# Three weight loads of the boot wait for matmuls, and ten more spare matmuls stand at its head

## The chip, the cores and the metric

The kernel runs on one core of a Trainium2 chip. The metric is the time of one execution in microseconds (us); lower is better. A core has five engines with queues of their own: PE (matmuls, with weight loads listed as PEld), DVE and ACT (elementwise work), POOL, and SP, which here only issues DMAs. Each engine works through its queue in order.

## The reference

Two layers follow each other: a recurrence over tokens with a decaying state (4 batches, 8 heads, 768 tokens, 48 channels a head), and a dense layer with the activation h - tanh(h) on its 3072 x 384 result.

```python
for t in range(S):                       # attention, per batch and head
    cur = einsum('bhd,bhe->bhde', u * k[t], v[t])
    y[t] = einsum('bhd,bhde->bhe', r[t], state + cur)
    state = w[t][:, None] * state + einsum('bhd,bhe->bhde', k[t], v[t])
x = y as (3072, 384)
h = x @ w_in                             # (384, 2048)
out = (h - tanh(h)) @ w_out              # (2048, 384)
```

## The kernel before

The tokens are split into eight blocks of 384 (four batches, two halves each). A block's recurrence is done in chunks of 64 tokens: running products of w ahead of and behind each token (pre and post, scans on DVE), scores inside a chunk (matmuls of 64 x 64, masked into the tile A), keys turned so that tokens lie on partitions (turn: PE transposes, then a copy to ks on ACT), updates of the state (update_1 on PE, update_2 on DVE), and results from scores and from states. The result, transposed, is xT, the input of the dense layer. The dense layer's hidden width is cut into 16 slices f of 128. While PE does the slices of block i, the engines prepare block i+1 in the gaps.

The order of work on PE, DVE, ACT and SP is written out by hand (a manual schedule); each engine takes its instructions in the order of the code, and waits are set where data flow from one engine to another. Only the first block has nothing to run beside: the function boot prepares it alone, and the main loop begins behind it.

In boot, SP issues in this order: w, k and r of both halves of the heads, v, then weight tiles. A weight tile is one slice f of w_in and w_out, 768 KB as 64-bit words. load_weights brings it into one of five raw buffers; convert makes three ACT operations of it (one to w_sb, two to up, all on L255) and one DVE operation (L259). more_weights issues the next load and puts it in the list raws, from which convert takes them in order. The first two tiles' ACT operations are run whole ahead of the results; of the third, two are run ahead of the copies of the results and one behind the first copies. begin_behind(ins, dma) makes a DMA wait for an instruction: the queue that issues it (SP) stops there until the instruction is done, and so do the DMAs behind it in that queue.

The steps of boot that matter, in the order of the code: six loads, v and three weight loads (L965 to L970); the first half's products, its turn and scores; the second half's; update_1 (L521, 96 matmuls); ACT's conversion of the first tile, with the fourth and fifth weight loads behind its third operation; results from the first half's scores (L603, 48 matmuls); update_2 on DVE; conversion of the second tile; results from states (L586) with the remaining scores (L447) between them; two operations of the third tile; copies of the results to late and xT (L636); small DMAs that fill the holes in xT from late (fill_holes, L643, three on SP and three on POOL); the next block's w (behind a copy), a sixth weight load; results from the second half's scores; more copies. Then the main loop begins with hp (L749).

Two helpers put matmuls on PE whose results nobody reads: busy (L269, 128 x 512) and passed (L277, 16 x 16). The argument ahead of turn is the number of the latter ahead of the boot's first transposes.

```python
def passed(to, n):
    by = ident.bitcast(BF16)[:, 0:16]
    for _ in range(n):
        nc.tensor.matmul(to[0:16, 0:16], lhsT=by, rhs=by, start=True, stop=True, skip_group_check=True)
```

Of the kernel before, what the change touches and what calls it, by code (L numbers as in the profile page):

```python
# [50 lines left out]
B, H, S, D = 4, 8, 768, 48  # L51
P = 128
L = 64
# [3 lines left out]
NCP = NCH // 2  # L57
# [63 lines left out]
def kernel(  # L121
# [12 lines left out]
    nc = tc.nc  # L134
# [29 lines left out]
    start = const.tile([P, UP * NCH * LP], F32, name="start", tag="start")  # L164
# [32 lines left out]
    A = const.tile([P, 2, NPAIR, NCP, L], F32, name="scores", tag="scores")  # L197
# [41 lines left out]
    def load_weights(f, queue):  # L239
        raw = conv.tile([P, 2 * DM, 2], I32, name="raw", tag="raw")  # L240
        ins = queue.dma_start(out=raw, in_=weights[f].bitcast(I32).rearrange("p (n two) -> p n two", two=2))
        return f, raw, ins

    def convert(f, raw, _):

        lo, hi = raw[:, :, 0], raw[:, :, 1]
        a = w_sb[:, f, :].bitcast(I32)
        up = conv.tile([P, 2 * DM], I32, name="up", tag="up", bufs=4)  # L250
        low, high = (up.bitcast(t).rearrange("p (n two) -> p n two", two=2)[:, :, i]
                     for i, t in enumerate((U16, F16)))

        def scaled(to, of, scale, bias=0.0):
            return lambda: nc.scalar.activation(out=to, in_=of, func=AF.Copy, scale=scale, bias=bias)  # L255

        return [scaled(a.bitcast(F32), hi.bitcast(F32), HIGH_SCALE), scaled(high, hi.bitcast(F32), SIGN_SCALE),
                scaled(low, lo.bitcast(U32), *LOW)], [
                lambda: nc.vector.scalar_tensor_tensor(out=a, in0=a, scalar=3, in1=up, op0=ALU.logical_shift_left,  # L259
                                                       op1=ALU.bitwise_or)]  # L260

    def scratch(ps):
        return ps.tile([P, 2, BANK], F32, name="att", tag="att")
# [17 lines left out]
    class Block:  # L281
# [177 lines left out]
        def own(self, ps, p0):  # L459
            return self.masked(ps, "k", "r", masks["diagonal"], p0)  # L460

        def earlier(self, ps, p0):
            return self.masked(ps, "post", "pre", masks["above"], p0)
# [41 lines left out]
        def update_1(self, ps):  # L505
            last = self.q == NQ - 1
            for cs in ((0, 1), (2,)):
                kvp = scratch(ps)
                for c in cs:
                    for par in range(2):  # L510
                        self.kv[2 * c + par] = kvp[:, par, (c - cs[0]) * NPAIR * D:(c - cs[0] + 1) * NPAIR * D]
                for p in reversed(range(NPAIR)):
                    for c in cs:
                        for h in range(2):
                            for par in range(2):
                                if last and 2 * c + par == NCH - 1:
                                    continue
                                toks = slice(64 * par, 64 * par + 64)
                                e0 = p * D2 + h * D
                                n0 = ((c - cs[0]) * NPAIR + p) * D  # L520
                                nc.tensor.matmul(kvp[64 * h:64 * h + 64, par, n0:n0 + D],  # L521
                                                 lhsT=self.ks[toks, p, c, 64 * h:64 * h + 64],
                                                 rhs=self.v[toks, c, e0:e0 + D], start=True, stop=True)

        def update_2(self):
            St = states[self.q]
# [66 lines left out]
        def from_scores(self, yp, slots, first, last):  # L593
            for n, slot in slots:
                for p in reversed(slot):
                    for c in range(NCP):
                        for h in range(2):
                            for par in range(2):
                                toks = slice(64 * par, 64 * par + 64)
                                e0 = 64 * (h ^ (p % 2))  # L600
                                f0 = p * D2 + h * D
                                n0 = (n * NCP + c) * L
                                nc.tensor.matmul(yp[p % 2][e0:e0 + D, par, n0:n0 + L],  # L603
                                                 lhsT=self.v[toks, c, f0:f0 + D],
                                                 rhs=A[toks, h, p, c, :],
                                                 start=(first and n == slots[0][0] and c == 0),
                                                 stop=(last and (n, c) == (slots[-1][0], NCP - 1)),
                                                 skip_group_check=True)

        def results(self, ps):  # L610
            self.yp = [scratch(ps) for e in range(2)]
# [2 lines left out]
        def result(self, part, pairs, last=False, more=False, **how):  # L614

            if self.begun and not self.more:
                nc.tensor.wait_ge(fence, len(fences))
            slots = [(p // 2, [x for x in pairs if x // 2 == p // 2]) for p in pairs if p % 2 == 0]  # L620
            getattr(self, part)(self.yp, slots, not self.begun, last, **how)
            self.begun, self.more = True, more
            if not last and not more:
                nc.tensor.drain().then_inc(fence, 1)
                fences.append(None)

        def result_out(self, pairs, copy=None):

# [323 lines left out]
    def more_weights(queue):  # L952
        raws.append(load_weights(more_weights.n, queue))
        more_weights.n += 1
        return raws[-1][-1]
# [3 lines left out]
    def begin_behind(ins, dma):  # L959
        tc.add_manual_dep(dma.ins, ins.ins.name, mybir.DependencyInfo(  # L960
            mybir.DependencyClass.Sync, mybir.DependencyReason.DATA))

    def boot(ps, blk, later):
        h1, h2 = HALVES
        for p0 in HALVES:  # L965
            for name in ("w", "k", "r"):
                blk.load(name, p0, UP)
        blk.load_v()
        for _ in range(3):
            more_weights(nc.sync)  # L970

        def run(ops):
            for op in ops:
                op()

        both = (h1, h1 + 1), (h2, h2 + 1)
        blk.behind(h1, UP)
        blk.take_whole(h1, UP)
        blk.before(h1, UP)
        blk.times_behind(h1, UP)  # L980
        blk.times_u(h1, UP)
        blk.turn(ps, h1, ahead=97)
        own = blk.own(ps, h1)
        blk.times_before(h1, UP)
        earlier = blk.earlier(ps, h1)
        blk.bound(h1)
        blk.bound(h2)
        blk.behind(h2, UP)
        blk.take_whole(h2, UP)
        own()  # L990
        blk.times_behind(h2, UP)
        blk.times_u(h2, UP)
        blk.turn(ps, h2)
        own = blk.own(ps, h2)
        earlier()
        blk.before(h2, UP)
        blk.times_before(h2, UP)
        blk.update_1(ps)
        first_a, first_b = convert(*raws.pop(0))
        second_a, second_b = convert(*raws.pop(0))  # L1000
        third_a, third_b = convert(*raws.pop(0))
        run(first_a[:2])
        begin_behind(first_a[2](), more_weights(nc.sync))
        more_weights(nc.sync)
        own()
        blk.results(ps)
        blk.result("from_scores", both[0])
        blk.update_2()
        run(second_a)
        blk.result("from_states", ALL, cs=(0, 1), more=True)  # L1010
        earlier = blk.earlier(ps, h2)
        run(third_a[:2])
        blk.result("from_states", ALL, cs=(2,))
        earlier()
        idle = scratch(ps)[:, 0]
        busy(idle, 2)
        blk.result_out((3,), nc.scalar.copy)
        blk.fill_holes([nc.sync, nc.gpsimd])
        begin_behind(blk.result_out((2,), nc.scalar.copy), later.load("w"))
        more_weights(nc.sync)  # L1020
        run(first_b)
        blk.result("from_scores", both[1], True)
        busy(idle, 5)
        run(third_a[2:])
        blk.result_out((1,), nc.scalar.copy)
        blk.result_out((0,), nc.vector.tensor_copy)
        later.load("k")
        fourth_a, fourth_b = convert(*raws.pop(0))
        run(fourth_a[:1])
        run(second_b)  # L1030
        run(third_b)
        blk.held(0, NPAIR)
        return fourth_a[1:], fourth_b
# [24 lines left out]
    for i, blk in enumerate(blocks):  # L1058
# [11 lines left out]
        phases, before, ahead, converted, loads = plan(i)  # L1070
# [3 lines left out]
        for f in range(NF):  # L1074
# [5 lines left out]
            h, made = first(here, f, ps_d)  # L1080
# [75 lines left out]
            while due and due[0][0] <= now:  # L1156
                _, add, what = due.pop(0)
# [84 lines left out]
```

## Time and profile before

| | us |
|---|---|
| median of three runs | 567.99 (567.37 to 569.71) |
| the profiled execution | 567.05 |
| its span, first to last instruction | 565.2 |
| PE busy | 546.4 (97%) |
| DVE busy | 477.3 (84%) |
| ACT busy | 376.8 (67%) |
| first hp matmul of the main loop starts | 27.87 |

Busy times count each engine's own instructions; DMA issues and waits are not counted. A line such as "16.67 0.81 ACT w_sb L255" in the chain of waits gives start, duration, engine, the tile written and the line of the code; the chain is followed back from the last instruction, at each step to whatever released it. In the timeline the text in square brackets is the engine's idle time before the row and what ended it. A tile's view ends with the times from issue to landing of the DMAs that write it. The three weight loads of the boot are issued from 4.5 to 7.2 us and land at about 14, 16 and 18 us; the fourth and fifth are issued at 19.4 and 19.8.

### The profile page before, as it was taken

The page shows a single profiled execution, that of the slowest core. Times are in us where ns is not written, and L with a number is a line of the kernel's source. Part 1 is how long each engine was busy: PE and PEld are TensorE (multiplying, and loading weights), DVE is VectorE, ACT ScalarE, POOL GpSimd, SP SyncE. Part 2 cuts the span into 40 slices and gives each one's busy share as a digit, 9 for nine tenths or more (in the row PEclk, how much of TensorE's full clock was granted, in tenths as well). Part 3 has the DMA queues.
Part 4 walks back from the last instruction along what each step waited for, and adds up shares of the span by engine and source line. Part 5 has one row for each costly group of instructions (what it writes and reads, how often), then busy time and mean ns, then how long its engine had stood idle before and what let it go on. Part 6 is the DMA issues. An engine that isn't in the chain of part 4 may idle for free.

```text
span 565.2 us, 13965 instructions
## 1 busy us (share of the span) xinstructions
PE 546.4 (97%) x5664; PEld 398.3 (70%) x5664; DVE 477.3 (84%) x926; ACT 376.8 (67%) x743; POOL 11.8 (2%) x40
## 2 busy tenths in 40 slices
PE   4889999999999999999999999999999999999996
PEld 4646666565665787877777777877877787787863
DVE  8888884799879989989999999989899998758673
ACT  3979893355337886588766886677865886566450
POOL 6100000000000000000000000000000000000000
PEclk9999999999999999999999999999999999999999
DMA  8596553244202532035302531126122320100101
GB/s 305 198 337 210 182 174 119 84 112 106 92 12 97 131 111 67 4 97 143 112 22 76 140 114 60 52 86 156 57 68 81 83 64 1 55 1 1 44 0 45
DMA packets 51268, 55.10 MB, mean 97 GB/s; under 512 B 21376, under 2 KB 49152, under 8 KB 51200
## 3 DMA queue, kind: packets, MB, share of 16 engines
q1 hardware_dynamic: 50960, 54.10, 31.6%
q8 instruction: 45, 0.74, 0.5%
q14 instruction: 23, 0.19, 0.1%
q0 software_dynamic: 96, 0.07, 0.1%
q10 hardware_dynamic: 144, 0.00, 0.0%
HBM read 43.55 MB, written 4.72 MB: 85 GB/s over the span
## 4 chain that ended last, share of the span: by engine, by line
PE 87%; DVE 6%; ACT 3%; DMA 2%; issue 1%; SPq 0%; DVEq 0%
PE hp L749 40%; PE acc L864 20%; PE acc L826 13%; PE att L864 5%; PE att L447 3%; PE att L586 2%; PE att L603 2%; PE att L521 2%; DVE g L796 1%; ACT up L255 1%; DMA r<-in_rT 1%; DMA w<-in_wT 1%; PE att L471 1%; DVE g L755 1%; DVE post L401 1%
## 5 line engine op out<-in xcount | busy, mean ns | idle before, releaser
L749 PE MATMUL hp<-xT,w_sb 128*128 128x384 f32 x768 | 270.1, 488 | 2.0 <-ACT h L752 1.4
L749 PEld LDWEIGHTS hp<-xT,w_sb 128*128 128x128 f32 x768 | 138.4, 190 | 81.8 <-ACT h L752 4.5
L752 ACT ACTIVATE h<-hp 128x384 f32<-128x384 f32 x128 | 62.8, 490 | 116.4 <-PE hp L749 114.7
L864 PE MATMUL acc<-forms,g 128*128 128x128 f32 x810 | 121.0, 277 | 0.5
L864 PEld LDWEIGHTS acc<-forms,g 128*128 128x128 f32 x810 | 109.1, 192 | 16.9 <-issue 1.2
L796 DVE TENSOR_TENSOR g<-g 128x256 f32<-128x256 f32 x225 | 95.4, 424 | 19.1 <-PE acc L864 0.5
L755 DVE SCALAR_TENSOR_TENSOR h<-h,s 128x384 f32<-128x384 f32 x128 | 70.3, 549 | 7.2 <-ACT s L770 6.6
L826 PE MATMUL acc<-w_sb,sums 128*128 128x384 f32 x192 | 68.1, 491 | 1.4 <-DVE sums L755 1.1
L755 DVE SCALAR_TENSOR_TENSOR g<-qa,h 128x384 f32<-128x384 f32 x96 | 53.6, 558 | 16.2 <-PE acc L864 2.7
L771 ACT ACTIVATE qa<-s,shift 128x384 f32<-128x384 f32 x90 | 55.4, 616 | 3.0
L773 ACT ACTIVATE junk<-s,shift 128x384 bf16<-128x384 f32 x90 | 54.0, 599 | 0.0
L826 PEld LDWEIGHTS acc<-w_sb,sums 128*128 128x128 f32 x192 | 35.7, 190 | 25.8 <-DVE sums L755 2.2
L770 ACT ACTIVATE s<-h 128x384 f32<-128x384 f32 x90 | 47.1, 523 | 2.8
L864 PE MATMUL acc<-w_sb,g 128*128 128x128 f32 x270 | 44.9, 275 | 0.0
L864 PEld LDWEIGHTS acc<-w_sb,g 128*128 128x128 f32 x270 | 37.4, 192 | 0.0
L781 ACT ACTIVATE qa<-s,shift 128x384 f32<-128x384 f32 x38 | 23.4, 617 | 19.3 <-DVE top L778 19.3
L255 ACT ACTIVATE up<-raw 128x768 f16<-128x768 f32 (+1 forms) x32 | 32.0, 1070 | 0.0
L755 DVE SCALAR_TENSOR_TENSOR sums<-qa,h 128x384 f32<-128x384 f32 x32 | 17.9, 558 | 15.6 <-ACT qa L781 12.4
L778 DVE CUSTOM_DVE_ANT_0 s<-h 128x384 f32<-128x384 f32 x38 | 21.0, 553 | 11.7 <-ACT h L752 11.7
L864 PE MATMUL att<-w_sb,g 128*128 128x128 f32 x180 | 30.2, 275 | 0.0
L864 PEld LDWEIGHTS att<-w_sb,g 128*128 128x128 f32 x180 | 26.4, 192 | 4.5
L387 DVE TENSOR_TENSOR_SCAN post<-w,seed 128x780 f32<-128x780 f32 x16 | 28.5, 1783 | 0.7 <-DMA w<-in_wT 0.6
(90 smaller groups left out, 549.3 us busy)
## 6 DMA issues: line engine op xcount, KB each, us to landing
raw<-in_weights SPq DMA_DIRECT2D x16, 768.0 KB, 4.4
w<-in_wT SPq DMA_DIRECT2D x7, 780.0 KB, 4.5
k<-in_kT SPq DMA_DIRECT2D x7, 768.0 KB, 4.4
r<-in_rT SPq DMA_DIRECT2D x7, 768.0 KB, 4.4
v_sb<-in_v SPq DMA_DIRECT2D x8, 576.0 KB, 4.3
k<-in_tokens SPq DMA_DIRECT2D x6, 576.0 KB, 3.9
r<-in_tokens SPq DMA_DIRECT2D x6, 576.0 KB, 4.8
out_y<-sums SPq DMA_DIRECT2D x15, 128.0 KB, 1.9
```

Source lines behind the costliest of these rows:

```text
L255: return lambda: nc.scalar.activation(out=to, in_=of, func=AF.Copy, scale=scale, bias=bias)
L387: return nc.vector.tensor_tensor_scan(out=back(t[:, 0:width]), data0=back(self.tile("w")[:, a:a + width]), data1=back(seed[:, 0:width]), i ...
L749: nc.tensor.matmul(hp, lhsT=w_in_sb[:, f, kc, :], rhs=xT[kc], start=(kc == KC - 1), stop=(kc == 0))
L752: return h, nc.scalar.activation(out=h, in_=hp, func=AF.Copy, scale=1.0 / UPSCALE)
L755: return lambda: nc.vector.scalar_tensor_tensor(out=out, in0=in0, scalar=scalar, in1=in1, op0=op0, op1=ALU.mult)
L770: nc.scalar.activation(out=s, in_=h, func=AF.Square)
L771: nc.scalar.activation(out=qa, in_=s, func=AF.Square, bias=shift[:, 4:5])
L773: nc.scalar.activation(out=junk[:, 0:NB], in_=s, func=AF.Relu, bias=shift[:, 5:6], accum_out=excess[:, at:at + 1])
L781: first = [lambda: nc.scalar.activation(out=qa, in_=s, func=AF.Square, bias=shift[:, 4:5])]
L796: return lambda: nc.vector.tensor_tensor(out=G[:, to:to + 2], in0=two(G, g_at(q, a0), g_at(q, a1)), in1=two(G, g_at(q, b0), g_at(q, b1)), ...
L826: nc.tensor.matmul(acc, lhsT=g[:, j * P:(j + 1) * P], rhs=w_out_sb[:, f, :], start=(f == self.first), stop=(f == NF - 1))
L864: nc.tensor.matmul(to, lhsT=G[:, g_at(q, a), :], rhs=rhs, start=start, stop=stop, skip_group_check=True)
```

## The change

The third weight load is no longer issued with the first two. It waits for the last matmul of update_1. The fourth waits for the last matmul of the results from the first half's scores, and the fifth follows it without a wait of its own; before, these two stood behind the third ACT operation on the first tile. To have something to wait for, update_1, from_scores and result return their last matmul. The spare matmuls ahead of the first turn are 107 instead of 97. The order of the instructions on ACT, DVE, POOL and SP stays as it was; on PE the ten matmuls and their weight loads are added at the head.

```diff
@@ update_1
-    nc.tensor.matmul(kvp[64 * h:64 * h + 64, par, n0:n0 + D], ...)
+    done = nc.tensor.matmul(
+        kvp[64 * h:64 * h + 64, par, n0:n0 + D], ...)
+            return done
@@ from_scores
-    nc.tensor.matmul(yp[p % 2][e0:e0 + D, par, n0:n0 + L], ...)
+    done = nc.tensor.matmul(
+        yp[p % 2][e0:e0 + D, par, n0:n0 + L], ...)
+            return done
@@ result
-            getattr(self, part)(self.yp, slots, not self.begun, last, **how)
+            done = getattr(self, part)(self.yp, slots, not self.begun, last, **how)
...
+            return done
@@ boot
-        for _ in range(3):
+        for _ in range(2):
             more_weights(nc.sync)
...
-        blk.turn(ps, h1, ahead=97)
+        blk.turn(ps, h1, ahead=107)
...
-        blk.update_1(ps)
+        updated = blk.update_1(ps)
         first_a, first_b = convert(*raws.pop(0))
         second_a, second_b = convert(*raws.pop(0))
+        begin_behind(updated, more_weights(nc.sync))
         third_a, third_b = convert(*raws.pop(0))
-        run(first_a[:2])
-        begin_behind(first_a[2](), more_weights(nc.sync))
-        more_weights(nc.sync)
+        run(first_a)
         own()
         blk.results(ps)
-        blk.result("from_scores", both[0])
+        begin_behind(blk.result("from_scores", both[0]), more_weights(nc.sync))
+        more_weights(nc.sync)
         blk.update_2()
         run(second_a)
```

More of the change, by code (lines that the diff above doesn't have):

```diff
@@ L520, in update_1 @@
                                 n0 = ((c - cs[0]) * NPAIR + p) * D
-                                nc.tensor.matmul(kvp[64 * h:64 * h + 64, par, n0:n0 + D],
-                                                 lhsT=self.ks[toks, p, c, 64 * h:64 * h + 64],
-                                                 rhs=self.v[toks, c, e0:e0 + D], start=True, stop=True)
+                                done = nc.tensor.matmul(
+                                    kvp[64 * h:64 * h + 64, par, n0:n0 + D],
+                                    lhsT=self.ks[toks, p, c, 64 * h:64 * h + 64],
+                                    rhs=self.v[toks, c, e0:e0 + D], start=True, stop=True)
+            return done
         def update_2(self):
@@ L602, in from_scores @@
                                 n0 = (n * NCP + c) * L
[L603 to L608, printed above, removed]
+                                done = nc.tensor.matmul(
+                                    yp[p % 2][e0:e0 + D, par, n0:n0 + L], lhsT=self.v[toks, c, f0:f0 + D],
+                                    rhs=A[toks, h, p, c, :], start=(first and n == slots[0][0] and c == 0),
+                                    stop=(last and (n, c) == (slots[-1][0], NCP - 1)), skip_group_check=True)
+            return done
         def results(self, ps):
```

## The prediction

> **What bounds the kernel now.** I read the page first, then the chain of waits from 14 to 42 us, then the timeline of the engines over the same stretch, then the landings of the weight loads. The page gives the frame:
>
> ```profile
> span 565.2 us, 13965 instructions
> ...
> PE 546.4 (97%) x5664; PEld 398.3 (70%) x5664; DVE 477.3 (84%) x926; ACT 376.8 (67%) x743; POOL 11.8 (2%) x40
> ...
> PE 87%; DVE 6%; ACT 3%; DMA 2%; issue 1%; SPq 0%; DVEq 0%
> ```
>
> PE carries the span, and from 42 us to the end its waits that the profile names add up to about 2 us. So the main loop can neither absorb nor return much. What the boot does to the moment at which PE gets steady work is passed on one to one. The edit touches only the boot, and there PE does not lead. Chain of waits, 14 to 42 us (start, duration, what):
>
> ```profile
> 15.87 0.80 ACT ks L473
> 16.67 0.81 ACT w_sb L255
> 17.48 1.88 ACT up L255 x2
> 19.36 0.74 ACT w_sb L255
> 20.10 1.88 ACT up L255 x2
> 21.98 0.78 ACT w_sb L255
> 22.76 0.96 ACT up L255
> 23.73 0.32 ACT late L636
> ...
> 27.29 4.54 DMA w<-in_wT
> 31.83 0.02 issue
> 31.85 1.79 DVE post L387
> ```
>
> The reader should see that from 15.87 to 27.29 us the chain is ACT and nothing else: the copy of the keys, three operations for the first weight tile, three for the second, two for the third, then the copies of the result. They stand in ACT's queue in this order, so a wait of one holds all that follow. The third tile's first operation is the row of 21.85 us in ACT's timeline, and it has no idle time before it: its load had landed long ago (at 6.7 us issued, 11.5 us to landing, so 18.2). PE's timeline shows what the changed loads will wait for:
>
> ```profile
> 15.77 1.56 PE L447 MATMUL att<-r,k 48*64 48x64 f32 x48
> 17.10 2.76 PE L521 MATMUL att<-v_sb,ks 64*64 64x48 f32 x96
> 19.64 1.46 PE L603 MATMUL att<-scores,v_sb 64*48 64x64 f32 x48
> ...
> 22.11 0.90 PE L447 MATMUL att<-pre,post 48*64 48x64 f32 x48
> ...
> 23.59 0.60 PE L269 MATMUL att<-ident 128*128 128x512 bf16 x2
> 24.59 0.55 PE L603 MATMUL att<-scores,v_sb 64*48 64x64 f32 x24 [0.40 <-ACT late L636]
> ```
>
> The updates (L521) end at 17.10 + 2.76 = 19.86 us, the first scores' results (L603) at 19.64 + 1.46 = 21.10. The last thing needed is how long a 768 KB weight load takes when the queue is quiet; tile raw, window 42 to 80 us, eight loads:
>
> ```profile
> DMA to landing us min/median/max: 3.9/4.2/4.3
> ```
>
> **The third load.** Its issue moves from 6.7 us to behind the last L521 matmul. The fourth load of before was issued at 19.38, 0.02 us after the ACT operation it waited for ended (17.48 + 1.88 = 19.36), so I take 19.86 + 0.02 = 19.88. With 4.2 us it lands at 24.1. ACT reaches the third tile at 21.85 as before, because everything ahead of it is unchanged, and now waits 24.1 - 21.85 = 2.25 us. Bounds: 3.9 us gives a stall of 1.95; the fourth load of before took 4.5 us from that very place, which gives 2.55. I take the median of the quiet loads, since the queue is empty at 19.9 (no bytes move from 18 to 20 us).
>
> **What is queued behind that wait.** On ACT: the third tile's second operation (22.65), the copies to late (23.57), to xT (24.57) and so all of the boot's end. DVE's copy of xT and PE's second scores (24.59, waiting for ACT late) stand behind them; so do the hole-filling DMAs on SP (24.57) and POOL (24.34), and behind these on SP the next block's load of w at 27.29, whose landing at 31.83 releases DVE's scan at 31.85. All of this moves by the same 2.25: w is issued at 29.54, lands 34.08, and the scan starts at 34.1. DVE had idled 0.64 us there for w, so neither engine has slack of its own. Nothing else comes late next: once the wait ends, ACT is again the chain.
>
> **The fourth and fifth loads.** They move from 19.38 and 19.76 to 21.12 and about 21.5, behind the third on the same queue. At about 400 GB/s (the windows from 22 to 24 us show 412 and 442) 768 KB take 1.9 us, so after the third at 24.1 they land at about 26.0 and 27.9. ACT used the fourth at 27.63, which becomes 29.88, and the fifth at 33.30, which becomes 35.5: 3.9 and 7.6 us of cover, so nothing. Without the ACT stall the cover of the fourth would still be 1.6 us. SP has nothing to issue between the fifth load (done by 22) and the hole-filling DMAs (26.8), so none of its other work is held. POOL's hole-filling DMAs share the engines with the loads: before, the fifth load landed 1.4 us after POOL's first was issued (19.76 + 6.0 against 24.34); now 27.9 against 26.6 is 1.3 us. No difference.
>
> **The spare instructions.** 97 take 2.58 us, so ten more take 10 x 2.58 / 97 = 0.27 us; PE then idled 4.55 us before its first turn. That idle time hides them: 0. If the cover were gone they would cost their 0.27. They also add 20 instructions to PE's stream. The queue q8 carried 45 packets of 0.74 MB together for PE's 11,328 matmuls and weight loads, one per 252. Each such packet now comes 20 instructions earlier in the stream. It can matter in one place: tile xT, and the DMA view from 25.2 to 26.2 us:
>
> ```profile
> L643 SPq DMA_DIRECT2D xT<-late x45: 518/582/1297, 24.6 to 486.3; - x45
> q8 instruction: 1, 0.02, 5.8%
> ```
>
> The second hole-filling issue of the boot is one of the long ones (1.30 us against a median of 0.58) and stands beside this packet; it pushes w's issue by 0.72. If the packet leaves that place, w comes 0.72 earlier; if it falls on another issue there, up to 0.72 later. I take 0, because the loads keep the queue full before the hole filling as they did before and the packet came out right behind them. [...]
>
> **Sum.** +2.25 us on the profiled execution's 567.05 (span 565.2 and 1.85 around it) is 569.3. The median of the three runs stands 0.94 above that execution, so the forecast in its terms is 567.99 + 2.25 = 570.2. From the terms' ends: 1.95 - 0.72 = +1.2, and 2.55 + 0.72 = +3.3, or 569.2 to 571.3.
>
> **Rival 1: PE falls back to its slow rate (slower by more).** Two groups of 48 like matmuls above (L447) took 1.56 us at 15.77 and 0.90 at 22.11: PE ran slower by 1.73 until about 21 us and at full rate after. With ACT stalled, PE has from 24.19 (end of L269) to 26.84 nothing to do, and then only 1.1 us of small matmuls until about 28.3. If that drops the rate, the five L269 matmuls (1.25 us) and the first hp (2.17) take 3.42 x 0.73 = 2.5 us more, less DVE's 0.64 of waiting for w: +1.9, in all +4.1 or 572.1; a drop for part of them gives +3 or so. It decides from the point at which 2.65 us of idle time count. For it: PE was slow in the boot after its 4.55 us of idle time. Against: it had been slow before that too, and after 21 us PE never idles over 1.1 us, so the profile is silent. [...]
>
> **Rival 2: the wait shrinks to nothing (not slower).** If the ten spare matmuls bring PE to full rate already before the second turn at 14.30, its six transposes take 0.73 us (twelve take 1.47 at 44.70) and not 1.54: ACT is 0.8 earlier. L521 follows on ACT's copy, at about 16.0, and takes 2.76 / 1.6 = 1.75, so the third load goes out at 17.8 and lands at 22.0, against ACT at 21.05: a stall of 0.95 less the 0.8 gained is +0.15. With the packet off the hole filling that becomes -0.6. So 567.4 to 568.1. It decides from PE's rate before 14 us. Against: 0.27 us more of tiny matmuls, 4.5 us ahead of the first turn, is little to bring that about.
>
> That the change does nothing can be excluded: in the built order SP's third load waits for PE, and ACT's third tile for that load.
>
> **How the numbers follow.** 0.5% is 2.84 us, about what a measurement of this kernel can tell from no change. The forecast has 0.58, of which 0.14 lies above +2.84, through a late landing or an added packet. Rival 1 has 0.22, all above. Rival 2 has 0.15, nearly all within. 0.05 is kept for a gain that I cannot derive: nothing in the boot can give 2.84 us back by these rows. That makes slower 0.14 + 0.22 = 0.36, same 0.44 + 0.14 = 0.58, faster 0.06. The range takes in the forecast's ends, most of rival 1 and the upper half of rival 2: 567.8 to 572.2.
>
> **What would show it.** Right: in the timeline of after, the third w_sb of ACT starts near 24.1 with some 2.2 us of idle time before it, put down to DMA raw; the third load's issue stands at 19.9; late moves to 25.8, w's issue to about 29.5, the scan to 34.1; the ten spare matmuls end at 4.92 with PE idle behind them. Rival 1 shows in the first hp group of six taking well over 2.2 us; rival 2 in L521 taking under 2 us. The prediction is wrong if ACT's third tile starts without a wait, if w's issue does not follow the late copy, or if DVE reaches the scan later than w lands.

## The result and the profile after

The changed kernel takes 570.13 us (median of 22 executions, 568.81 to 571.65), the kernel before beside it 567.47 us (22 executions, 566.84 to 569.83). The ratio, worked out from all executions, is 1.0042, with a 95% interval of 1.0032 to 1.0051: slower by about 2.4 us; the medians alone stand 2.66 us apart. The forecast was 570.2 us: +2.25 us on a kernel before that stood at 567.99 us. In the runs beside the experiments below about a third of the executions of the kernel before lie 1.5 us or more above their median, so there a difference of medians can be a microsecond or more above what the ratio says.

The profiled execution of the changed kernel took 569.13 us, 2.08 us more than that of before. The page after:

```profile
span 567.3 us, 13985 instructions
PE 546.0 (96%) x5674; PEld 396.7 (70%) x5674; DVE 477.2 (84%) x926; ACT 376.9 (66%) x743; POOL 11.9 (2%) x40
```

No engine has more work than before; PE is even 0.4 us less busy. The time went into waiting. The chain of waits after, 14 to 45 us (start, duration, what), has a load where before it had only ACT:

```profile
18.83 4.48 DMA raw<-in_weights
...
23.33 0.90 ACT w_sb L255
...
25.18 0.32 ACT late L638
```

ACT's timeline after shows the same from the waiting engine's side:

```profile
19.51 1.98 ACT L255 ACTIVATE up<-raw 128x768 f16<-128x768 f32 x2
23.33 0.90 ACT L255 ACTIVATE w_sb<-raw 128x768 f32<-128x768 f32 x1 [1.84 <-DMA raw<-in_weights]
24.14 1.04 ACT L255 ACTIVATE up<-raw 128x768 f16<-128x768 f32 x1
25.05 0.94 ACT L638 COPY late<-att 48x384 f32<-48x384 f32 x2
```

ACT came to the third tile at 21.49 us (23.33 - 1.84), 0.36 before its place in the kernel before, and stood there 1.84 us for a load issued at 18.83. The copies to late start at 25.05 instead of 23.57: +1.48. PE's timeline after, from the second turn to the first hp:

```profile
14.38 0.87 PE L471 MATMUL att<-ident,post 128*128 128x128 f32 x6 [1.03 <-DVE post L401]
...
15.93 1.44 PE L521 MATMUL att<-v_sb,ks 64*64 64x48 f32 x86
18.37 0.37 PE L521 MATMUL att<-v_sb,ks 64*64 64x48 f32 x9 [1.00 <-issue]
...
26.05 0.55 PE L605 MATMUL att<-scores,v_sb 64*48 64x64 f32 x24 [2.15 <-ACT late L638]
27.05 0.89 PE L605 MATMUL att<-scores,v_sb 64*48 64x64 f32 x24 [0.44 <-ACT xT L638]
27.87 2.28 PE L269 MATMUL att<-ident 128*128 128x512 bf16 x5
30.39 2.17 PE L751 MATMUL hp<-xT,w_sb 128*128 128x384 f32 x6 [0.24 <-DVE w_sb L259]
```

Before, two of these rows were:

```profile
26.07 1.25 PE L269 MATMUL att<-ident 128*128 128x512 bf16 x5
27.87 2.17 PE L749 MATMUL hp<-xT,w_sb 128*128 128x384 f32 x6 [0.54 <-DMA xT<-late]
```

Three things are to be seen. PE was at full rate already in the second turn (0.87 us for the six transposes, 1.54 before), so the updates ended and the third load went out a microsecond early, in spite of a gap of 1.00 us ahead of the last ten updates. PE then idled 2.15 us for the stalled ACT. Behind that PE fell to half rate: the second scores took 0.55 and then 0.89 us for like groups, and the five L269 matmuls 2.28 us where before they took 1.25. The windows confirm it (length, then PE, PEld, DVE, ACT and POOL busy, the granted clock, DMA share, GB/s); after:

```profile
23.00:26.50 3.50, 1.22 (x38) 0.53 (x28) 1.70 (x2) 3.12 (x5) 0.70 (x2) 1.00 0.94 367
26.60:29.90 3.30, 2.86 (x30) 1.27 (x29) 1.78 (x3) 3.21 (x5) 0.78 (x2) 0.50 0.35 78
```

Before:

```profile
23.00:26.50 3.50, 2.54 (x87) 1.45 (x76) 2.08 (x4) 3.40 (x6) 1.71 (x5) 1.00 0.61 232
```

In the first window after PE was busy for 1.22 us of 3.5; in the next one the granted clock was 0.50. Before, PE was busy 2.54 us of the same stretch, and the clock stayed at 1.00.

The first hp starts at 30.39 instead of 27.87, +2.52. What counts in the end is DVE's scan (L387), which waits for the later of two things, the next block's w and the first hp's way through ACT and DVE (h, then s). DVE's timeline after:

```profile
33.18 0.56 DVE L780 CUSTOM_DVE_ANT_0 s<-h 128x384 f32<-128x384 f32 x1 [2.03 <-ACT h L754]
...
33.66 1.78 DVE L387 TENSOR_TENSOR_SCAN post<-w,seed 128x780 f32<-128x780 f32 x1
```

Before, this scan waited for w:

```profile
31.85 1.78 DVE L387 TENSOR_TENSOR_SCAN post<-w,seed 128x780 f32<-128x780 f32 x1 [0.64 <-DMA w<-in_wT]
```

Now w (issued 28.43, 4.68 in flight) had landed at 33.11, and the scan followed s without a wait for w, at 33.66: +1.81. The matmuls acc (L828) follow the scan by 8.87 to 8.89 us in both kernels (40.72 before, 42.55 after), and the first hp of the next block is also 1.83 late (101.27 against 99.44). So the boot's loss stands at 1.8 us at the scan, and the span ends 2.1 later.

### The profile page after: what moved, and what is told of

The parts are those of the page before. It is cut to its first block, busy times and chain, and to the rows that moved or that the text cites. A ratio compares the mean times of both kernels' runs of the same rounds, so it can differ in the third digit from the quotient of the medians.

```text
span 567.3 us, 13985 instructions
## 1 busy us (share of the span) xinstructions
PE 546.0 (96%) x5674; PEld 396.7 (70%) x5674; DVE 477.2 (84%) x926; ACT 376.9 (66%) x743; POOL 11.9 (2%) x40
## 4 chain that ended last, share of the span: by engine, by line
PE 87%; DVE 8%; ACT 2%; issue 2%; DMA 1%; DVEq 0%; SPq 0%; ACTq 0%
PE hp L751 40%; PE acc L866 20%; PE acc L828 13%; PE att L866 5%; PE att L447 3%; PE att L521 2%; PE att L588 2%; PE att L605 2%; DVE g L798 1%; DVE post L387 1%; DVE g L757 1%; DVE post L401 1%; DMA raw<-in_weights 1%; PE att L471 1%; DVE states L545 1%
## 5 line engine op out<-in xcount | busy, mean ns | idle before, releaser
L828 PE MATMUL acc<-w_sb,sums 128*128 128x384 f32 x192 | 68.0, 490 | 0.7 <-DVE sums L757 0.5
L828 PEld LDWEIGHTS acc<-w_sb,sums 128*128 128x128 f32 x192 | 35.7, 190 | 25.0 <-DVE sums L757 1.1
L783 ACT ACTIVATE qa<-s,shift 128x384 f32<-128x384 f32 x38 | 23.3, 614 | 18.6 <-DVE top L780 18.6
L866 PEld LDWEIGHTS att<-w_sb,g 128*128 128x128 f32 x180 | 26.4, 192 | 4.5
L376 DVE TENSOR_TENSOR_SCAN pre<-w,start 128x780 f32<-128x780 f32 x16 | 28.5, 1782 | 0.6
```

Of the source, the lines that this page charges most:

```text
L376: return nc.vector.tensor_tensor_scan(out=self.tile("pre")[:, cols], data0=self.tile("w")[:, cols], data1=start[:, 0:n * NCH * LP], initia ...
L783: first = [lambda: nc.scalar.activation(out=qa, in_=s, func=AF.Square, bias=shift[:, 4:5])]
L828: nc.tensor.matmul(acc, lhsT=g[:, j * P:(j + 1) * P], rhs=w_out_sb[:, f, :], start=(f == self.first), stop=(f == NF - 1))
L866: nc.tensor.matmul(to, lhsT=G[:, g_at(q, a), :], rhs=rhs, start=start, stop=stop, skip_group_check=True)
```

## The experiments

The table gathers the readings of one profiled execution of each kernel, in us: when the third load landed, how long ACT waited for it, when the fifth load and POOL's second hole-filling DMA landed, the first hp, the landing of w, the scan. The last column is the median less that of the kernel before, run beside it on the same chip (567.82 for e1 to e4, 567.91 for e5 to e8, 567.98 for e9 to e12; 12 executions of each experiment). The profiled execution is one of the twelve and need not be like their median: it is the slowest of e1, the fastest of e2 and e5, and the second fastest of e4 and e12.

| | 3rd | ACT waits | 5th | holes | first hp | w | scan | median |
|---|---|---|---|---|---|---|---|---|
| before | 18.2 | 0 | 25.8 | 27.62 | 27.87 | 31.83 | 31.85 | |
| after | 23.3 | 1.84 | 29.6 | 30.15 | 30.39 | 33.11 | 33.66 | +2.66 |
| e1 | 25.6 | 3.67 | 30.8 | 31.36 | 32.62 | 35.0 | 36.61 | +2.45 |
| e2 | 18.0 | 0 | 27.8 | 28.40 | 28.64 | 31.8 | 31.91 | +0.23 |
| e3 | 18.9 | 0 | 28.5 | 29.01 | 29.25 | 32.5 | 32.52 | +1.20 |
| e4 | 23.0 | 0 | 28.7 | 29.23 | 29.48 | 32.0 | 34.40 | +3.42 |
| e5 | 22.7 | 1.33 | 27.7 | 28.23 | 28.53 | 32.44 | 32.47 | +1.61 |
| e6 | 20.5 | 0 | 26.4 | 28.29 | 28.54 | 32.12 | 32.14 | -0.11 |
| e7 | 23.9 | 1.92 | 29.1 | 29.68 | 30.49 | 33.2 | 34.29 | +2.53 |
| e8 | 18.4 | 0 | 22.1 | 29.89 | 31.59 | 34.3 | 34.85 | +2.44 |
| e9 | 18.0 | 0 | 26.4 | 27.68 | 28.36 | 31.85 | 31.87 | +0.27 |
| e10 | 22.8 | 1.79 | 28.9 | 29.41 | 29.66 | 32.6 | 32.92 | +0.91 |
| e11 | 19.9 | 0 | 27.3 | 27.84 | 28.09 | 31.2 | 31.36 | -1.06 |
| e12 | 23.1 | 0 | 33.0 | 27.55 | 27.80 | 31.1 | 31.09 | -0.22 |

Three rules hold down the table. The first hp starts 0.24 to 0.25 us after the landing of POOL's second hole-filling DMA in nine rows (before, after, e2 to e4, e6, e10 to e12); in e1, e7 and e8 it comes later, 0.10 to 0.11 us after the slow L269 matmuls end, and in e5 and e9 the profile has it wait for ACT's copy of xT. The scan starts at the later of w's landing and 3.27 us after the first hp, where that hp group runs at full rate (28.64 + 3.27 = 31.91 in e2; in after 30.39 + 3.27 = 33.66); in e1, e4 and e7 the group itself took 2.70 to 3.83 us for 2.17, and the scan came later still. The span is the scan plus 533.3 to 534.2 us. So the scan shows what the boot costs in the profiled execution.

**e1: the third load alone.** The kernel before, with only the third load moved behind the updates; the fourth and fifth stay behind the first tile's third operation, and there are 97 spare matmuls.

```diff
-        for _ in range(3):
+        for _ in range(2):
             more_weights(nc.sync)
...
-        blk.update_1(ps)
+        updated = blk.update_1(ps)
...
+        begin_behind(updated, more_weights(nc.sync))
         third_a, third_b = convert(*raws.pop(0))
```

> Before, with the third load alone moved behind the updates; the fourth and fifth stand behind the first tile's third operation as before, 97 spare matmuls. Theory (ACT waits for the third load, all else is free): ACT idles 1.8 to 2.6 us before the third tile and the kernel is 2.0 to 2.6 us slower than before, the whole of the change. Rival (the fourth and fifth loads, which land up to 3.9 us later in the changed kernel and keep the queue full when the hole filling starts, carry it): under 1 us slower.

Measured: 570.27 us (569.2 to 572.12), ratio 1.0022 (0.9998 to 1.0047). ACT's timeline in e1, and the landings of the three loads issued from 19.9 to 21.6 us (tile raw):

```profile
25.68 0.89 ACT L255 ACTIVATE w_sb<-raw 128x768 f32<-128x768 f32 x1 [3.67 <-DMA raw<-in_weights]
```

```profile
DMA to landing us min/median/max: 5.7/7.4/9.2
```

The moved third load alone brings ACT's wait, in this execution (the slowest of the twelve) a longer one than in the change: the load took 5.7 us to land where a lone one takes about 4.2. The two loads right behind it are not shown to be the reason, as in e7 the third load lands in 4.1 us with two as close behind. PE idled 4.15 us and its clock stood at 0.50 from 27.3 to 34.1. The medians are apart by what was expected; the ratio says less and its interval still touches 1, but the wait stands in the trace.

**e2: the fourth and fifth alone.** The kernel before, with the third load at the head as it was, and the other two behind the first scores' results.

```diff
-        run(first_a[:2])
-        begin_behind(first_a[2](), more_weights(nc.sync))
-        more_weights(nc.sync)
+        run(first_a)
         own()
         blk.results(ps)
-        blk.result("from_scores", both[0])
+        begin_behind(blk.result("from_scores", both[0]), more_weights(nc.sync))
+        more_weights(nc.sync)
```

> Before, with the fourth and fifth loads alone moved behind the first scores' results; the third is issued early, 97 spare matmuls. Theory: no stall on ACT, within 0.5 us of before. Rival (the later loads carry it): 1 us or more slower, with the holes in xT filled late and the first hp waiting for them.

Measured: 568.05 us (567.44 to 570.12), ratio 0.9999 (0.9979 to 1.0020). ACT's timeline in e2 has the third tile without a wait:

```profile
21.41 0.90 ACT L255 ACTIVATE w_sb<-raw 128x768 f32<-128x768 f32 x1
```

This part of the change, without the late third load, costs nothing that could be measured, though the holes are filled 0.8 us later than before and the first hp is as late.

**e3: the spare matmuls alone.** The kernel before with ten more.

```diff
-        blk.turn(ps, h1, ahead=97)
+        blk.turn(ps, h1, ahead=107)
```

> Before, with 107 spare matmuls for 97 and nothing else. Theory: they end at 4.9 us in PE's idle time, within 0.3 us of before. Rival (20 more instructions move PE's instruction packets off or onto the hole filling, or bring the full clock earlier): 0.5 us or more away from before, either way.

Measured: 569.02 us (566.83 to 572.8), ratio 1.0013 (0.9988 to 1.0038): no difference shown, and not excluded. In the trace PE idles behind the 107 as it did behind the 97. The scan is 0.67 us late in its profiled execution, in which the first w landed 1.1 us later than before (5.2 against 4.1) and the weight loads 0.7 later (15.2, 17.1, 18.9); the rows show nothing that ties this to the ten matmuls.

**e4: the third tile behind the copies.** The changed kernel, with ACT's operations on the third tile moved behind the copies of the results, so that nothing urgent stands behind the wait.

```diff
-        run(third_a[:2])
         blk.result("from_states", ALL, cs=(2,))
...
-        run(third_a[2:])
         blk.result_out((1,), nc.scalar.copy)
+        run(third_a)
```

> The changed kernel, with the three ACT operations of the third tile run behind the boot's last ACT copy of results instead of ahead of the first one; the loads wait as in the changed kernel. Theory (the loss is ACT standing still ahead of the copies): ACT does not wait, the copies start near 23.5 us, and the kernel comes to within 0.1 to 0.8 us of before (the third tile itself is ready some 2 us later, just when its hp wants it). Rival (the loss comes from the transfers or from PE's clock): it stays about 2 us or more slower than before.

Measured: 571.24 us (567.84 to 572.42), ratio 1.0034 (1.0010 to 1.0057). The expected gain did not come; the time is the rival's. ACT's copies start at 23.17 without a wait for the load, as meant, but in PE's timeline of e4 the first hp is only 0.9 us earlier than in the change:

```profile
25.68 1.25 PE L269 MATMUL att<-ident 128*128 128x512 bf16 x5
29.48 3.83 PE L751 MATMUL hp<-xT,w_sb 128*128 128x384 f32 x6 [2.55 <-DMA xT<-late]
```

Its wait is now for the small hole-filling DMAs. They were issued from 23.9 us, but landed only after 4.3 to 5.0 us (1.9 to 2.9 before), right behind the fifth weight load, which landed at 28.7. Behind those 2.55 us the clock fell here too (0.50 from 29.8 to 33.2), and the first hp group took 3.83 us for 2.17. One wait was taken away, and the next one stood directly behind it.

**e12: and the fifth load last.** e4, with the fifth load moved behind the next block's w.

```diff
         begin_behind(blk.result("from_scores", both[0]), more_weights(nc.sync))
-        more_weights(nc.sync)
...
         more_weights(nc.sync)
+        more_weights(nc.sync)
         run(first_b)
```

> The kernel with the third tile's conversion behind the copies, and now the fifth load behind the next block's w too, so that it does not stand ahead of the hole filling. Theory (there the first hp waited for holes filled behind the fifth load): the holes land within 2.5 us of their issue, the first hp's wait for them falls from 2.5 us to under 0.8, and the kernel gains 1.5 us or more on the one without this, to within 1.2 us of before. Rival (the third tile's lateness itself is the loss): no gain.

Measured: 567.76 us (567.08 to 571.43), ratio 0.9994 (0.9972 to 1.0016), its median 3.5 us under that of e4. PE's timeline in e12:

```profile
27.80 2.17 PE L751 MATMUL hp<-xT,w_sb 128*128 128x384 f32 x6 [0.89 <-DMA xT<-late]
```

The hole-filling DMAs landed in 2.6 to 3.3 us and the wait is 0.89; both are a little longer than expected, but the scan is at 31.09. So e4's loss was the fifth load ahead of the holes, with the fall of the clock behind it. And the third load as late as in the change (landed at 23.1) costs nothing that could be measured, if nothing urgent queues behind its consumer.

**e5: PE kept busy.** The changed kernel with twelve L269 matmuls for two, to cover the idle time.

```diff
-        busy(idle, 2)
+        busy(idle, 12)
```

> The changed kernel with 12 instead of 2 spare 128x512 matmuls where PE waits for the late copy: some 2.2 us of idle time filled, nothing else moved. Theory (ACT's wait of about 2 us carries the loss): 1.6 us or more slower than before still; the granted clock stays full through the boot's end, as PE no longer idles, and that is worth at most 0.5 us. Rival (PE's half clock after the idle time carries it, rival 1 of the prediction): within 0.7 us of before.

Measured: 569.52 us (568.21 to 570.12), ratio 1.0009 (0.9988 to 1.0030). The windows of e5, for the stretch that ran at 0.50 in the change:

```profile
26.60:29.90 3.30, 2.96 (x33) 1.53 (x30) 2.72 (x4) 2.77 (x4) 0.18 (x1) 1.00 0.44 78
```

The clock stayed at 1.00, and in PE's timeline the five L269 matmuls take 1.25 us again. Part of the loss stays: the medians are 1.6 us above before, where the changed kernel is 2.7 above. So the loss is just at the least that the theory allowed, and the gain of about 1 us over the change is twice what it granted the clock. But this execution, the fastest of the twelve, had a shorter wait too (1.33 us), and the fifth load and the holes landed 1.9 us sooner, so it does not price the half rate alone.

**e6: the third load earlier.** The changed kernel, with the third load behind the second turn's copy of the keys instead of behind the updates.

```diff
-        blk.turn(ps, h2)
+        keys = blk.turn(ps, h2)
+        begin_behind(keys, more_weights(nc.sync))
```

> The changed kernel with the third load behind ACT's second copy of keys (some 3 us earlier) instead of behind the updates; fourth and fifth behind the first scores' results, 107 spare matmuls. Theory: the load lands near 21.0 us, before ACT wants it at 21.4 to 21.9, ACT does not wait, and the kernel is within 0.5 us of before. Rival (any load in the middle of the boot costs, or the later fourth and fifth do): 1.5 us or more slower than before.

Measured: 567.8 us (566.79 to 569.78), ratio 0.9978 (0.9955 to 1.0002). The load goes out at 16.4 and lands at 20.5, and ACT's timeline in e6 has no wait:

```profile
21.61 0.92 ACT L255 ACTIVATE w_sb<-raw 128x768 f32<-128x768 f32 x1
```

With everything else of the change in place, 2.4 us of earlier issue take the whole loss away.

**e7: the third load later.** The changed kernel, with the third load behind the first scores' results and the other two right behind it.

```diff
-        updated = blk.update_1(ps)
+        blk.update_1(ps)
...
-        begin_behind(updated, more_weights(nc.sync))
-        third_a, third_b = convert(*raws.pop(0))
...
         more_weights(nc.sync)
+        more_weights(nc.sync)
+        third_a, third_b = convert(*raws.pop(0))
         blk.update_2()
```

> The changed kernel with the third load too behind the first scores' results, so 1.2 us later than in the changed kernel, fourth and fifth directly behind it. Theory: ACT's wait grows by that and the kernel is 1.0 to 2.0 us slower than the changed one, 3.2 to 4.5 us slower than before (the upper end if three loads side by side land later than one alone). Rival (something other than ACT's wait sets the end): no slower than the changed kernel.

Measured: 570.44 us (569.63 to 572.33), ratio 1.0036 (1.0013 to 1.0058). This was meant as a higher dose, 1.0 to 2.0 us more than the change, and it missed: ACT waited 1.92 us, only 0.08 more, and the loss by the medians is no larger (2.53 against 2.66). The load went out 0.94 us later than in the change, but ACT came to the tile 0.48 later (21.97), and the load took 4.10 us for 4.48. With the same wait, the same loss; the dose that was to be tested did not come about.

**e8: all five loads at the head.** The kernel before with no load waiting for anything.

```diff
-        for _ in range(3):
+        for _ in range(5):
             more_weights(nc.sync)
...
-        run(first_a[:2])
-        begin_behind(first_a[2](), more_weights(nc.sync))
-        more_weights(nc.sync)
+        run(first_a)
```

> Before, with all five weight loads issued at once at the head, 97 spare matmuls. Theory: no load is late and the queue is empty when the holes are filled, so that these land about 2 us after their issue: 0 to 0.7 us faster than before. Rival (the early transfers delay the loads of w, k and r or the instruction packets, which is why two were held back): 0.5 us or more slower.

Measured: 570.35 us (569.79 to 571.15), ratio 1.0028 (1.0005 to 1.0050): slower, though ACT waits for no load. PE's timeline in e8, then ACT's, then the DMA queues from 18.5 to 19.8 us:

```profile
21.24 1.53 PE L603 MATMUL att<-scores,v_sb 64*48 64x64 f32 x48 [1.34 <-issue]
```

```profile
26.77 0.97 ACT L636 COPY late<-att 48x384 f32<-48x384 f32 x2 [3.04 <-PE att L586]
```

```profile
q8 instruction: 1, 0.02, 5.2%
```

With the weight loads keeping the data queue full (q1 102.2% from 15 to 18.5 us), this packet of instructions came at 18.64, where it came between 15.2 and 16.9 in the other kernels, and PE stood 1.34 us with nothing that the profile can name. The gap is not e8's alone: after, e2 to e6, e11 and e12 have one of 0.4 to 1.5 us ahead of the same instruction, the 700th of PE's matmuls and weight loads, and in all of them, e8 too, it ends 2.2 to 2.6 us after that packet began. That PE waited for instructions there, in e8 longer than in most and later, is an estimate from these times. Its clock came up only at about 31 us (five L269 matmuls took 1.88 us at 29.61). The copies to late waited for PE.

**e9, e10 and e11: spare work meant to bring PE to full rate from the head.** Each has ten L269 matmuls behind the 97 spare ones: e9 is the kernel before with them; e10 is the changed kernel, e11 is e6, both with 97 for 107 spare matmuls, and e10 also has e5's twelve.

```diff
             passed(tp[:, 0], ahead)
+            if ahead:
+                busy(tp[:, 0], 10)
```

e10 and e11 against the changed kernel and e6, and e10 alone:

```diff
-        blk.turn(ps, h1, ahead=107)
+        blk.turn(ps, h1, ahead=97)
```

```diff
-        busy(idle, 2)
+        busy(idle, 12)
```

> Before, with ten spare 128x512 matmuls behind the 97 small ones at the head, so that PE works from 2 to about 9 us where it idled 4.5 us. Theory (part of the executions lose time because PE's clock comes late or falls back in the boot): the granted clock is 0.997 or more in nearly all executions, and the median falls by 0.5 to 1.5 us against before. Rival (the clock is not what spreads them, or PE at full clock only waits for its instructions): no faster than before, or slower.

> The changed loads with the clock's part taken away on both sides: 97 small and ten 128x512 spare matmuls at the head, and 12 instead of 2 where PE waits for the late copy. Theory (a pure wait of ACT for the third load is left, smaller because PE at full clock finishes the updates some 1 us earlier): 1.0 to 2.0 us slower than the kernel with the same head and the loads of before. Rival (the loss was the clock's alone): within 0.5 us of it.

> The third load behind the second copy of keys, as in the run that did so, with 97 small and ten 128x512 spare matmuls at the head. Theory: no wait on ACT and a full clock; 0.5 to 1.5 us faster than before, the best of all. Rival: no better than before.

Measured: e9 568.25 us (566.56 to 572.45), ratio 1.0001 (0.9972 to 1.0031); e10 568.89 (567.82 to 570.12), 0.9994 (0.9974 to 1.0013); e11 566.92 (566.24 to 567.58), 0.9967 (0.9948 to 0.9986). The gain expected of e9 did not come: six transposes took 0.87 us in its first turn but 1.54 again in its second, behind 2.2 us of idle time, and none of its executions reached the mean clock of 0.997. The half rate lasted from 13.6 to 20.4 us in e9 and from 15.0 to 18.4 in e10, so the head did not hold the clock in either. Against e9, the comparison that was meant, e10 is 0.64 us slower by the medians, between its theory and its rival, and not shown to differ. e10 and e11 differ in e5's twelve matmuls and in the moment of the third load; in the profiled executions e11's clock also stayed full. ACT waits 1.79 us in the one and not at all in the other, the scans are 1.56 apart, the medians 1.97, and no execution of e11 is as slow as the fastest of e10. That is the best measure of the third load's lateness, and e11 is the one version shown to be faster than before. Its first hp still waits for the holes, which again stand behind the fifth load (27.3):

```profile
28.09 2.17 PE L753 MATMUL hp<-xT,w_sb 128*128 128x384 f32 x6 [1.60 <-DMA xT<-late]
```

## Why the prediction came out right

The forecast of the total was right, and its root is shown: the third load lands late, ACT waits for it in order, and the result copies, the holes and w move with it. e1 brings the loss by the medians with this part alone, e2 has the rest without it and no loss, e6 takes the loss away by an earlier issue. But 570.2 against 570.13 is partly luck. The medians rose by 2.66 us, not 2.25, from a kernel before that stood 0.52 lower than in the forecast; and the terms inside partly cancelled.

**The third load's wait, +2.25: mis-sized, 1.84 measured.** Flight time was 4.48 us, not 4.2. The issue was at 18.83, not 19.88, and ACT was there 0.36 early, because PE was at full rate before the second turn. Less these 0.36, and 0.34 for quicker issues on SP, w went out 1.14 late and landed 1.28 late (4.68 us in flight against 4.54).

**The fourth and fifth loads, "no difference": this step failed.** By the prediction the fifth was to land 1.3 us after POOL issued its first hole-filling DMA; it landed 3.8 us after (29.61 against 25.80), 9.4 us after its own issue. The hole-filling DMAs then took 3.4 to 4.0 us, and the first hp started at 30.39, 0.24 us after POOL's second: 2.52 late, a microsecond more than the copies. In nine kernels (after, e1 to e5, e7, e10, e11) that DMA lands 0.5 to 0.6 us after the fifth load, and in e12, with the fifth out of the way, it takes 3.0 us for e4's 4.7. The profile names DVE's w_sb for the hp's wait in after, but in before that same operation ended at 28.4, when the hp had begun, so it cannot be what hp needs.

The holes were not alone in this. In after the five slow L269 matmuls ended at 30.15 too, at the moment of that landing. In e1, e7 and e8 the first hp follows them by 0.10 to 0.11 us, so with the holes on time it would have started at about 30.26, only 0.13 us sooner (an estimate). Each of the two is seen alone: in e10, with these matmuls at full rate, the holes put the scan 0.36 us behind w's landing; in e7 the half rate holds the first hp back 0.8 us after the landing.

The step was saved in part by slack: before, hp reached the scan 0.71 us ahead of w (27.87 + 3.27 = 31.14 against 31.85), so of 2.52 only 1.81 came through, 0.53 more than w alone would have brought. Whether the change makes the fifth slow is open: in e3, where it stands as before, it took 8.2 us, and in e6, where it stands as in the change, 6.0. The DMA engines as a whole were not full at its end: from 26.6 to 29.9 us they were busy 0.35 of the time and moved 78 GB/s.

**"Neither engine has slack": wrong, in the form that the prediction named as a sign of being wrong.** DVE reached the scan later than w landed; the 0.64 us of waiting for w was slack for the hp path and was used up.

**Rival 1, PE at half rate: it came beside the forecast, not in its place.** The clock fell, and took 1.03 us more for the five L269 matmuls; the first hp group ran at full rate (2.17). What it cost in the profiled execution cannot be told from the holes, which came to PE at the same moment. In e1, e4 and e7 it struck the hp group (2.90, 3.83 and 2.70 us); in e4 that was 1.66 us. e5, with PE kept busy, is about 1 us better than the change by the medians. In after the clock fell behind 2.15 us of unbroken idle time, in a stretch of 3.5 us (23.0 to 26.5) with 1.22 us of work.

**Rival 2, full rate before the second turn: its premise came true, not its result or its reason.** The transposes took 0.87 us, but the updates then had a gap of 1.00 us in which PE waited for nothing named, so the load went out at 18.83 and not at 17.8. The ten spare matmuls are not the cause of the full rate: e2 and e6 show 0.88 with 97 and with 107, e1 and e7 show 1.54 with 97 and with 107.

**The spare instructions and their packet: taken at 0, with one place overlooked.** The prediction looked at the hole filling, but the gap of 1.00 us is ahead of PE's 700th instruction. With the ten matmuls this falls ahead of the last ten updates, for which the third load waits; in e2, with 97, it falls behind all of them. So at full rate they put the third load off by about the gap, an estimate: no run has the changed loads with 97 spare matmuls at full rate. e3, whose third load is early, cannot show it, and has no difference clear of noise. The long issue on SP moved to another hole-filling DMA and shrank from 1.30 to 0.99 us, within the bounds of 0.72.

So 1.28 through w, 0.53 more through the first hp (holes and half rate together), and 0.27 behind the scan (2.08 - 1.81) make the 2.08 of the profiled executions. The last term, and the rest up to the 2.66 of the medians, are not traced to a cause.

## What to carry to other kernels

Cost a delayed load from its consumer's place in an in-order queue: issue plus flight (4.1 to 4.6 us for the moved loads here, 5.7 in one execution) against the moment at which the consumer gets there, and then ask which two paths meet behind it and how much slack the earlier one has. Look at what small, urgent transfers stand behind a large one that nobody needs yet: moving that one back was worth 3.5 us by the medians from e4 to e12. Issuing everything as early as possible is no safe answer either, as e8 shows.

## What the runs showed of the hardware

- Three weight loads of 768 KB issued within 1.7 us landed 5.7, 7.4 and 9.2 us after their issue (e1), and three within 1.1 us in 4.1, 5.6 and 8.3 (e7); the lone ones take 3.9 to 4.3. From like places the fifth load took between 6.0 us (before, e6) and 9.4 us (after); what decides is open.
- PE stood 0.4 to 1.5 us ahead of its 700th matmul or weight load in nine kernels, 1.34 us in e8 with the data queue full (102.2% by q1 from 15 to 18.5 us), but also 1.00 us in after, where no DMA moved a byte from 17.2 to 18.4 us. In all nine a packet of q8 began 2.2 to 2.6 us before PE went on; whether PE waited for it, the profile does not name.
- The half rate lasted 3.41 us in after, e4, e7 and e10, and 6.83 in e1 and e9. Cut into stretches of 3.41 us, PE's time at full rate up to about 40 us has six, over all 14 traces, in which PE was busy for 1.52 us or less, and the clock fell behind each of them (after: 1.13 us from 23.16 to 26.57); behind all others, with 1.81 us or more, it stayed full. In these traces the fall went with PE's busy share of such a stretch, not with the length of one wait: ahead of the second turn PE idled 2.22 us in e10 and in e11, and the clock fell after it in e10 alone.
- The moment at which PE reaches full rate differs between executions and kernels: the second turn's six transposes took 0.87 to 0.88 us in after, e2 to e6 and e10 to e12, and 1.54 in before, e1, e7, e8 and e9.
